# One-pass making of weight words, scores ahead of their bias, and plain copies that a planner may give to ScalarE or VectorE

## Chip, cores and metric

The kernel runs on one core of a Trainium2 chip. The metric is the device time of one execution in microseconds, 1084.62 us for the kernel before (median of three runs, 1083.74 to 1085.63).

## What is computed

The reference is a chain of an attention and two feed-forward layers:

```
scores = q @ k.T / sqrt(64) - slope[h] * dist, kept where the key is global or in the local window
x   = softmax(scores) @ v                    # 4 batches, 8 heads, 768 positions, head size 64
h   = x @ w_in
x   = (h * cos(h)) @ w_out                   # 3072 tokens, 512 -> 2048 -> 512
out = relu(x @ w2_in) ** 2 @ w2_out          # 3072 tokens, 512 -> 2048 -> 512
```

The four weight matrices arrive in double precision. The kernel makes a float32 word of each double from its two 32-bit halves, and splits the result into two fp16 parts, a high and a low one, so that TensorE multiplies in fp16 with three products for each block.

## The kernel before

The 3072 tokens are 24 tiles (T) of 128, four to each of six blocks (b). Layer 1 (m = 0) and layer 2 (m = 1) go block by block through a sequence of twelve stages, the first of which is layer 1 of block 0. That stage needs the attention of tiles 0 to 3 whole, and the weights of layer 1 pair by pair as it goes on.

`fast_path` does not issue instructions as it goes: each piece of work is an entry of a `Plan` with the engines that may do it, a cost, a due time and the buffers that it reads and writes. `Plan.run` then gives every engine its order, earliest due first, and a table `SHIFTS` moves the due times of attention tiles (A, P, X) and weights (W). An entry with one way has one engine; `split_lo` entries (the low fp16 part, a subtraction) may go to VectorE (DVE) or GpSimd (POOL). Each engine then works through its order strictly, so a late instruction holds up what stands behind it. Where the planner sees TensorE idle for over 0.9 us in the first 240 us, `idle_products` puts in products with a tile of zeros (`nought`).

What the change touches:

- `build_bias` (L494 to L519) makes a table of distances on DVE; `head_bias` (L523) makes from it the eight heads' biases on ScalarE (ACT).
- `group32` does the scores of four heads of tiles 0 to 3 in fp32: `add_bias` (L871) puts the bias into PSUM by a product with the identity, the score products (L788) add to it, `largest` takes the maximum (L878) and scales it (L882) on DVE, `expo_from` (L886) takes the exponentials on ACT, `diagonal` (L799 to L803) makes a diagonal of the reciprocal sums, products with it turn the tile (L816), ACT copies the turned tile out of PSUM (L821), products with v follow (L831), and ACT copies the result to SBUF (L840). There are eight such groups ahead of the first feed-forward product (L1125).
- `split_x`, `split_kq` and `weight` make a high part by an ACT copy to fp16 (L860, L696, L571; 1024 columns) and the low part by `split_lo` (L474).
- `decoded` loads 1 MB of doubles into one of two `raw` buffers (L558) and makes 1024 float32 words a partition from them: ACT's `magnitude` (L56), then three DVE passes, `join_steps`: a shift (L62), the low word's bits (L65), the sign (L68). The second and third read `raw`, so the buffer comes free after L68. 16 such units are made for layer 1 in the first 160 us and 16 for layer 2 later.

## Time and profile before

| | |
|---|---|
| median of the runs | 1084.62 us |
| the profiled execution | 1085.72 us, span 1084.0 us |
| TensorE (PE) busy | 1060.6 us, 98% of the span |
| DVE busy | 802.8 us, 74% |
| ACT busy | 752.9 us, 69% |
| POOL busy | 245.1 us, 23% |
| chain that ended last | PE 83%, DVE 11%, ACT 4% |

PE busy times are of pipelined matmuls with modelled ends, so a busy PE need not be doing useful products. In the rows further on, a stretch's PEclk is the clock that the throttle granted as a share of full speed, and in a timeline the bracket names the idle time before the instruction and what ended it.

### The profile page before, as it was taken

The numbers are of one execution on the slowest core, as the hardware profiler recorded it, in microseconds if no ns is written. First come the engines' busy times: TensorE is split into PE (matmuls) and PEld (weight loads), VectorE is DVE, ScalarE is ACT, GpSimd is POOL, SyncE is SP. The second block draws the span as 40 slices with busy tenths as digits, with TensorE's granted clock in tenths as the row PEclk, the third lists the DMA queues.
The fourth block names the chain that finished last, engine by engine and source line by source line (L and its number), as shares of the span: only waits on it lengthen the run. The fifth ranks groups of instructions, "written<-read, shape, count | busy, mean of one in ns | idle before, by whom it ended". The sixth has DMA issues, their size and how long they took to land.

```text
span 1084.0 us, 23236 instructions
## 1 busy us (share of the span) xinstructions
PE 1060.6 (98%) x9380; PEld 753.3 (69%) x9380; DVE 802.8 (74%) x1483; ACT 752.9 (69%) x1349; POOL 245.1 (23%) x192
## 2 busy tenths in 40 slices
...
GB/s 234 171 243 250 238 282 246 152 97 238 229 177 209 295 338 157 246 226 229 249 272 261 233 232 222 268 315 255 195 216 135 127 137 127 128 117 156 86 4 41
DMA packets 160687, 217.69 MB, mean 201 GB/s; under 512 B 110464, under 2 KB 110976, under 8 KB 159040
## 3 DMA queue, kind: packets, MB, share of 16 engines
...
## 4 chain that ended last, share of the span: by engine, by line
PE 83%; DVE 11%; ACT 4%; issue 1%; DMA 0%; DVEq 0%; SPq 0%; ACTq 0%
PE hps L1232 25%; PE ypps L1141 14%; PE hps L1125 13%; PE ypps L1368 11%; PE ypps L1438 7%; PE ypps L1183 7%; PE hps L922 2%; PE hps L983 2%; PE hps L1368 2%; DVE dec L65 1%; DVE nm L878 1%; DVE dec L68 1%; DVE dec L62 1%; DVE t L1426 1%; DVE xy L474 1%
## 5 line engine op out<-in xcount | busy, mean ns | idle before, releaser
L1232 PEld LDWEIGHTS <-ld 128*128 128x128 f16 x2400 | 234.0, 98 | 35.3 <-issue 2.6
L1232 PE MATMUL hps<-ys,ld 128*128 128x256 f16 x1680 | 195.1, 273 | 1.8 <-DVE t L1426 1.8
L1141 PE MATMUL ypps<-g,ld 128*128 128x512 f16 x768 | 177.8, 382 | 1.6 <-DVE g L474 1.6
L1125 PE MATMUL hps<-xy,w 128*128 128x512 f16 x768 | 174.5, 379 | 0.0
L1426 DVE TENSOR_TENSOR t<-hps,t 128x512 f32<-128x512 f32 x160 | 110.0, 688 | 66.4 <-PE hps L1232 64.3
L1141 PEld LDWEIGHTS <-ld 128*128 128x128 f16 x768 | 74.3, 98 | 90.2 <-issue 2.7
L1125 PEld LDWEIGHTS <-w 128*128 128x128 f16 x768 | 73.9, 98 | 86.2
L474 DVE TENSOR_TENSOR g<-t,g 128x512 f16<-128x512 f32 (+1 forms) x128 | 101.0, 793 | 26.0 <-ACT g L1209 25.2
L1209 ACT ACTIVATE g<-t 128x512 f16<-128x512 f32 x128 | 79.3, 622 | 23.5 <-DVE t L1165 21.8
L1183 PE MATMUL ypps<-g,ld 128*128 128x256 f16 x768 | 89.2, 273 | 0.5 <-DVE g L474 0.5
L1438 PE MATMUL ypps<-ld,g 128*128 128x512 f16 x384 | 89.5, 379 | 0.0
L1183 PEld LDWEIGHTS <-ld 128*128 128x128 f16 x768 | 75.0, 98 | 9.4 <-issue 0.6
L1423 ACT ACTIVATE t<-t 128x512 f32<-128x512 f32 x72 | 45.0, 624 | 48.9 <-DVE t L1426 48.6
L474 POOL TENSOR_TENSOR g<-t,g 128x512 f16<-128x512 f32 (+1 forms) x24 | 30.8, 1284 | 195.0 <-ACT g L1209 185.1
L1165 DVE SCALAR_TENSOR_TENSOR t<-t,hps 128x512 f32<-128x512 f32 x72 | 48.9, 682 | 31.9 <-ACT t L1163 31.9
L1161 ACT ACTIVATE t<-hps 128x512 f32<-128x512 f32 x72 | 42.7, 592 | 34.0 <-PE hps L1125 25.4
L1438 PEld LDWEIGHTS <-g 128*128 128x128 f16 x384 | 36.7, 98 | 37.1
L1163 ACT ACTIVATE t<-t 128x512 f32<-128x512 f32 x96 | 60.4, 629 | 2.6
L1258 ACT ACTIVATE t<-t 128x512 f32<-128x512 f32 x96 | 60.3, 628 | 2.5
L954 ACT ACTIVATE e<-e,nm 128x256 f32<-128x256 f32 (+1 forms) x128 | 52.7, 482 | 8.3 <-DVE nm L946 8.1
L946 DVE CUSTOM_DVE_ANT_0 e<-hps,bias 128x256 f32<-128x256 f32 (+2 forms) x128 | 43.2, 395 | 18.0 <-PE hps L922 17.9
L631 POOL TENSOR_TENSOR t<-t 128x256 f32<-128x256 f32 x18 | 16.4, 909 | 158.0 <-DVE x L631 157.9
...
## 6 DMA issues: line engine op xcount, KB each, us to landing
...
raw<-w SPq DMA_DIRECT2D x32, 1024.0 KB, 6.6
...
yd<-xy SPq DMA_DIRECT2D x6, 1024.0 KB, 5.8
xy<-yd SPq DMA_DIRECT2D x6, 1024.0 KB, 6.6
...
```

Source lines behind the costliest of these rows:

```text
L474: op.emit = lambda: eng[op.eng].tensor_tensor(out=out_f(), in0=src_f(), in1=hi_f(), op=ALU.subtract)
L954: nc.scalar.activation(out=at(e)[:, x, 0:W], in_=at(e)[:, x, 0:W], func=ACTF.Exp, bias=at(nm)[:, x:x + 1], scale=-1.0,)
L1125: nc.tensor.matmul(out=at(ps), lhsT=w_view(wt)[:, a, j % 2, k * 128:(k + 1) * 128], rhs=x_view(src)[:, c, k, :], start=(n == 0), stop=(n = ...
L1141: nc.tensor.matmul(out=at(y_ps[d]), lhsT=wv[:, a, d * 128:(d + 1) * 128], rhs=at(g)[:, c], start=(j == 0 and n == 0), stop=(j == NJ - 1 an ...
L1163: act(due + 1.2, 512, lambda: nc.scalar.activation(out=at(t), in_=at(t), func=ACTF.Square, scale=HALF_TURN), w=[t])
L1183: nc.tensor.matmul(out=at(y_ps[d])[:, 256 * n:256 * n + 256], lhsT=w_view(wt)[:, a, u, d * 128:(d + 1) * 128], rhs=at(g)[:, z, 256 * u:256 ...
L1209: act(due, 512, lambda: nc.scalar.activation(out=at(g)[:, 0], in_=at(t), func=ACTF.Copy), r=[t], new=[g])
L1232: nc.tensor.matmul(out=at(bank)[:, 256 * u:256 * u + 256], lhsT=wv(a, u, kk), rhs=sv(c, kk), start=(fresh and u == n == 0), stop=(last and ...
L1258: act(due, 512, lambda: nc.scalar.activation(out=at(t), in_=at(t), func=ACTF.Square), w=[t])
L1368: nc.tensor.matmul(out=at(bank)[:, 256 * half:256 * half + 256], lhsT=gv(home)[:, z, c0:c0 + 128], rhs=wv(a, u), start=(q == half == u == ...
L1426: dve(due, 0.7, lambda: nc.vector.tensor_tensor(out=at(t), in0=at(bank), in1=at(u), op=ALU.add), port=False, **k)
L1438: nc.tensor.matmul(out=at(y_ps[d]), lhsT=at(g)[:, z, 256 * u + d % 2 * 128:256 * u + d % 2 * 128 + 128], rhs=wv[:, a, u], start=(q == i == ...
```

## The change

- **Words.** The load lands one 16-bit word further into `raw`, so that the upper 16 bits of a double and the 32 bits below them each stand aligned. ACT's `top_half` (new L62) reads the upper 16 bits as bf16, scales, and writes an fp16 number into the upper half of a word of a new tile `top`, of which there is one; its lower halves are cleared once at the start. One DVE pass, `join` (new L69), ors in the middle bits. Shift and sign pass are gone. `raw` comes free after `join`.
- **Copies.** `cast` replaces the ACT copies named above (L571, L696, L821, L840, L860, the copies of attention probabilities and of g) by entries that the planner gives to ACT or to DVE (new L495 and L497). The scaling of the maximum is an entry of its own, `scaled`, for DVE, POOL or ACT (new L893, L891).
- **Beginning.** The scores are multiplied first and the bias added last, as two entries; heads 0, 1, 4 and 5 get their bias first; the cast of n_global and n_local comes two instructions later on DVE; the copies for the global keys wait for the last bias; the fp32 identity is gone.
- `SHIFTS` has other numbers. The counts of products, loads and stores are otherwise as they were.

```diff
@@ -49,29 +49,26 @@
 H_MOST = 3.0
-W_MAG = 2.0 ** -111
-def magnitude(nc, t, r):
-    nc.scalar.activation(out=t.bitcast(FP32), in_=r[:, :, 1].bitcast(FP32), func=ACTF.Abs, scale=W_MAG)
-def join_steps(nc, t, r):
-    return (
-        lambda: nc.vector.tensor_scalar(
-            out=t, in0=t, scalar1=3, scalar2=None, op0=ALU.logical_shift_left
-        ),
-        lambda: nc.vector.scalar_tensor_tensor(
-            out=t, in0=r[:, :, 0], scalar=29, in1=t, op0=ALU.logical_shift_right, op1=ALU.bitwise_or
-        ),
-        lambda: nc.vector.scalar_tensor_tensor(
-            out=t, in0=r[:, :, 1], scalar=-0x80000000, in1=t, op0=ALU.bitwise_and, op1=ALU.bitwise_or
-        ),
-    )
+INT16 = mybir.dt.int16
+UP = S_W ** 0.125
+def shifted(r, n):
+    return r.bitcast(INT16)[:, 1:4 * n + 1]
+def top_half(nc, t, r, n):
+    nc.scalar.activation(
+        out=t.bitcast(FP16).rearrange("p (c b) -> p c b", b=2)[:, :, 1],
+        in_=r.bitcast(BF16)[:, 4:4 * n + 4].rearrange("p (c b) -> p c b", b=4)[:, :, 0], func=ACTF.Copy, scale=UP)
+def join(nc, f, t, r, n):
+    nc.vector.scalar_tensor_tensor(
+        out=f, in0=r[:, 0:2 * n].rearrange("p (c b) -> p c b", b=2)[:, :, 1], scalar=13, in1=t,
+        op0=ALU.logical_shift_right, op1=ALU.bitwise_or)
 AHEAD = 2.0
@@ -82,51 +79,62 @@
...
-    ('A', 0, 0): 7.9,
+    ('A', 0, 0): -2.8,
...
-    ('W', 0, 0): -18.2,
+    ('W', 0, 0): -6.6,
...
+EITHER = 10.0
+BEGIN = 1.3
+RATE = 320.0
@@ -337,7 +346,7 @@
                                 held.append(item)
                                 break
                         elif ok and e == "DVE":
-                            k = o.due + (SHARED if len(o.ways) > 1 else 0.0) + (BESIDE if port and beside else 0.0)
+                            k = o.due + (0.0 if len(o.ways) == 1 else EITHER if o.ways[0][0] == "ACT" else SHARED) + (BESIDE if port and beside else 0.0)
                             if pick is None or k < key:
                                 pick, key = (o, way), k
                             if key <= o.due:
@@ -427,7 +436,7 @@
     kinds = dict(
-        raw=(2, [128, 1024, 2], INT32), ld=(9, [128, 1024], FP32), ys=(4, [128, 2048], FP16), kq=(3, [128, 2, 2, HR, 128], FP16), 
...
@@ -477,6 +485,20 @@
     def act(due, n, fn, **k):
         return plan.add((("ACT", (n + 230) / 1200, False),), due, fn, **k)
+    def cast(due, n, out, src, psum=False, **k):
+
+        us = (n + 150) / 960 if psum else (n / 2 + 150) / 960
+        o = plan.add((("ACT", (n + 230) / 1200, False), ("DVE", us, not psum)), due, None, **k)
+
+        def fn():
+            if o.eng == "ACT":
+                nc.scalar.activation(out=out(), in_=src(), func=ACTF.Copy)
+            else:
+                nc.vector.tensor_copy(out=out(), in_=src())
+
+        o.emit = fn
+        return o
+
     def own(b, first):
@@ -513,10 +533,13 @@
         nc.vector.tensor_scalar(out=t, in0=rel, scalar1=0.0, scalar2=BIG, op0=ALU.is_lt, op1=ALU.mult)
         nc.vector.tensor_tensor(out=t, in0=t, in1=rel, op=ALU.add)
+        nc.vector.tensor_copy(out=nf, in_=n_raw[:, :, 0])
...
         nc.vector.scalar_tensor_tensor(out=t, in0=col, scalar=nf[:, 1:2], in1=t, op0=ALU.max, op1=ALU.min)
+
+        nc.gpsimd.memset(slots["top"][0], 0)
...
@@ -553,22 +576,20 @@
     def decoded(m, e, jj, due):
-        t, raw = new("dec"), new("raw")
-        r = lambda: at(raw)
+        f, t, raw = new("dec"), new("top"), new("raw")
         dma(due - 12, 1024, lambda: nc.sync.dma_start(
-            out=r().rearrange("p (u a) b -> p u (a b)", u=2),
-            in_=w[m, e, 2 * jj:2 * jj + 2].bitcast(INT32).rearrange("u p c -> p u c")), new=[raw])
-        act(due - 7, 1140, lambda: magnitude(nc, at(t), r()), r=[raw], new=[t])
-        for n, us in enumerate((0.69, 1.22, 1.22)):
-            dve(due - 5.6 + 1.3 * n, us, lambda n=n: join_steps(nc, at(t), r())[n](), r=[raw] if n else [], w=[t])
-        return t
+            out=shifted(at(raw), 1024).rearrange("p (u c) -> p u c", u=2),
+            in_=w[m, e, 2 * jj:2 * jj + 2].bitcast(INT16).rearrange("u p c -> p u c")), new=[raw])
+        act(due - 7, 1024, lambda: top_half(nc, at(t), at(raw), 1024), r=[raw], new=[t])
+        dve(due - 5.6, 1.22, lambda: join(nc, at(f), at(t), at(raw), 1024), r=[t, raw], new=[f])
+        return f
     def weight(m, e, jj, due):
         t = decoded(m, e, jj, due)
         o = new("w1" if m == e == 0 else "ld")
         f = lambda: at(t).bitcast(FP32).rearrange("p (u c) -> p u c", u=2)
         ov = lambda: w_view(o)
-        act(due - 2.2, 1024, lambda: nc.scalar.activation(out=ov()[:, 0], in_=f(), func=ACTF.Copy), r=[t], new=[o])
+        cast(due - 2.2, 1024, lambda: ov()[:, 0], f, r=[t], new=[o])
         split_lo(o, due - 1.2, lambda: ov()[:, 1], f, lambda: ov()[:, 0], 1024, [t], [o])
         if m == 0:
...
@@ -780,18 +800,21 @@
         rows = (slice(0, D), slice(D, 128))
         def scores():
-            add_bias(ps, g, adds)
             for i in range(2):
                 c = 2 * g + i
-                for o, kk, c0, n in keys:
+                for n0, (o, kk, c0, n) in enumerate(keys):
                     for r in range(2):
                         nc.tensor.matmul(
                             out=at(ps[r])[:, 256 * i + o:256 * i + o + n], lhsT=f4(f)[rows[r], 1, c, :],
-                            rhs=f4(kk)[rows[r], 0, c, c0:c0 + n], start=False, stop=True, skip_group_check=True,
+                            rhs=f4(kk)[rows[r], 0, c, c0:c0 + n], start=(i == n0 == 0), stop=False, skip_group_check=True,
                         )
-        plan.add((("PE", 2.0, False),), s, scores, r=reads, new=ps, lag=0.3, after=[biased[h] for h in heads])
+        k = dict(part=reads) if T == g == 0 else dict(r=reads)
+        plan.add((("PE", 1.3 if t else 0.65, False),), s, scores, new=ps, lag=0.3, **k)
+        plan.add((("PE", 0.65, False),), s + 0.5, lambda: add_bias(ps, g, adds, last=True), w=ps, lag=0.3,
+                 after=[biased[h] for h in heads])
         dve(s + 1, 1.4 * W / 256, lambda: largest(ps, nm, W), port=False, r=ps, new=[nm])
+        scaled(nm, s + 2.5)
         act(s + 3, 1980 if t else 1460, lambda: expo_from(ps, e, nm, W, sums), r=ps, w=[nm], new=[e, sums], tab="exp")
         op = dve(s + 5, 1.1, None, r=[sums], new=[diag])
@@ -818,8 +841,7 @@
                     )
             plan.add((("PE", 1.2, False),), s + 7 + k, turned, r=[e, diag], new=[tp], lag=0.3)
-            act(s + 8 + k, 512, lambda tp=tp, pt=pt: nc.scalar.activation(
-                out=at(pt), in_=at(tp), func=ACTF.Copy), r=[tp], new=[pt])
+            cast(s + 8 + k, 512, lambda pt=pt: at(pt), lambda tp=tp: at(tp), psum=True, r=[tp], new=[pt])
             pts.append(pt)
         blocks = [v32[T - 1], v32[T]] if t else [v32[T]]
...
-    def add_bias(ps, g, adds):
+    def scaled(nm, due):
+
+        o = plan.add((("DVE", 0.17, True), ("POOL", 0.2, True), ("ACT", 0.21, False)), due, None, w=[nm])
+
+        def fn():
+            if o.eng == "ACT":
+                nc.scalar.activation(out=at(nm), in_=at(nm), func=ACTF.Copy, scale=-SCALE)
+            else:
+                eng[o.eng].tensor_scalar(out=at(nm), in0=at(nm), scalar1=-SCALE, scalar2=None, op0=ALU.mult)
+
+        o.emit = fn
+
+    def add_bias(ps, g, adds, last=False):
         for r in range(2):
@@ -870,7 +902,7 @@
             for n, (c0, c1, b0) in enumerate(adds):
                 nc.tensor.matmul(
                     out=p[:, :, c0:c1], lhsT=ident, rhs=bias[:, h0:h0 + 2, b0:b0 + c1 - c0],
-                    start=(n == 0), stop=False, skip_group_check=True,
+                    start=(n == 0 and not last), stop=last, skip_group_check=True,
                 )
...
-        nc.vector.tensor_scalar(out=at(nm), in0=at(nm), scalar1=-SCALE, scalar2=None, op0=ALU.mult)
...
@@ -1532,9 +1563,10 @@
         fill(3, at_(13))
-    dist_of = dve(0.0, 4.0, build_bias, r=[], after=())
-    for h in range(H):
-        biased.append(act(4.0 + PAIR * (h // 2), 320, lambda h=h: head_bias(h), after=[dist_of]))
+    dist_of = dve(0.0, 5.4, build_bias, r=[], after=())
+    biased = {}
+    for n, h in enumerate((0, 1, 4, 5, 2, 3, 6, 7)):
+        biased[h] = act(4.0 + PAIR * (n // 2), 215, lambda h=h: head_bias(h), after=[dist_of])
     for T in range(BT):
         attend32(T)
```


Three places show what it does to the orders. The first is TensorE's very first instructions; `hps` are PSUM banks, `ld` loaded tiles, `ident` the identity. Before:

```order
L871 LDWEIGHTS ident
L871 MATMUL hps_138<-bias,ident 128x2x224
L871 LDWEIGHTS ident
L871 MATMUL hps_138<-bias,ident 128x2x32
L871 LDWEIGHTS ident
L871 MATMUL hps_139<-bias,ident 128x2x224
L871 LDWEIGHTS ident
L871 MATMUL hps_139<-bias,ident 128x2x32
L788 MATMUL hps_138<-ld_72 128x128
L788 MATMUL hps_139<-ld_72 128x128
L788 MATMUL hps_138<-ld_70,ld_72 128x128
L788 MATMUL hps_139<-ld_70,ld_72 128x128
```

and now:

```order
L807 MATMUL hps_139<-ld_71 128x128
L807 MATMUL hps_140<-ld_71 128x128
L807 MATMUL hps_139<-ld_71 128x128
L807 MATMUL hps_140<-ld_71 128x128
L903 LDWEIGHTS ident
L903 MATMUL hps_139<-bias,ident 128x2x96
L903 LDWEIGHTS ident
L903 MATMUL hps_139<-bias,ident 128x2x32
L903 LDWEIGHTS ident
L903 MATMUL hps_140<-bias,ident 128x2x96
L903 LDWEIGHTS ident
L903 MATMUL hps_140<-bias,ident 128x2x32
```

The bias products of the first group stood ahead of its scores and now stand behind them, and the first group is that of tile 0 (keys of its own tile alone) where it was tile 1's.

The second is DVE around the first units of weights, some 30 instructions in; `w_0` is the high and low part of the first weights, `sm` sums, `xy` the attention's result, `t` a turned tile. Before:

```order
L62 TENSOR_SCALAR dec_109<-dec_109 128x1024
L65 SCALAR_TENSOR_TENSOR dec_109<-raw_68,dec_109 128x1024
L878 TENSOR_REDUCE nm_94<-hps_140 128x2
L878 TENSOR_REDUCE nm_94<-hps_141 128x2
L882 TENSOR_SCALAR nm_94<-nm_94 128x4
L68 SCALAR_TENSOR_TENSOR dec_109<-raw_68,dec_109 128x1024
L799 TENSOR_SCALAR sm_97<-sm_97 128x4
L802 RECIPROCAL sm_97<-sm_97 128x4
L803 TENSOR_TENSOR t_123<-ident_197,sm_97 128x512
L703 SCALAR_TENSOR_TENSOR v_87<-ld_73,v_87 128x8x64
L1547 COPY v_87<-vg_90 32x16x64
```

and now:

```order
L69 SCALAR_TENSOR_TENSOR dec_110<-raw_69,top_68 128x1024
L497 CAST w_0_112<-dec_110 128x1024
L822 TENSOR_SCALAR sm_96<-sm_96 128x4
L825 RECIPROCAL sm_96<-sm_96 128x4
L826 TENSOR_TENSOR t_120<-ident,sm_96 128x512
L482 TENSOR_TENSOR w_0_112<-dec_110,w_0_112 128x1024
L69 SCALAR_TENSOR_TENSOR dec_111<-raw_70,top_68 128x1024
L910 TENSOR_REDUCE nm_93<-hps_141 128x2
L910 TENSOR_REDUCE nm_93<-hps_142 128x2
L497 COPY xy_107<-ypps_145 128x2x128
L482 TENSOR_TENSOR w_1_113<-dec_111,w_1_113 128x1024
L497 COPY t_124<-ypps_146 128x512
```

One `join` stands for the three passes of a unit, and between the groups' instructions there are now copies to fp16 (`w_0`) and out of PSUM (`xy`, `t`) that ACT did. No scaling of `nm` stands there.

The third is ACT's first work; `vg` and `kg` are the global values and keys, `bias` the biases of the eight heads. Before:

```order
L753 ACTIVATE vg_90<-ld_71 32x8x64
L523 ACTIVATE bias<-dist 128x320 x8
L696 ACTIVATE kq_83<-ld_73 128x1024
L748 ACTIVATE kg_89<-ld_70 128x128
L701 ACTIVATE v_86<-ld_75 128x8x64
L886 ACTIVATE e_99,sm_95<-hps_138,nm_91 128x256 x2
L886 ACTIVATE e_99,sm_95<-hps_139,nm_91 128x256 x2
L886 ACTIVATE e_100,sm_96<-hps_140,nm_92 128x128 x2
```

and now:

```order
L546 ACTIVATE bias<-ys_80 128x320 x8
L773 ACTIVATE vg_91<-ld_73 32x8x64
L917 ACTIVATE e_100,sm_96<-hps_139,nm_92 128x128 x2
L917 ACTIVATE e_100,sm_96<-hps_140,nm_92 128x128 x2
L720 ACTIVATE v_87<-ld_75 128x8x64
L768 ACTIVATE kg_90<-ld_71 128x128
L891 ACTIVATE nm_93<-nm_93 128x4
L917 ACTIVATE e_101,sm_97<-hps_141,nm_93 128x128 x2
```

The exponentials of the first group now follow two instructions after the biases; a copy of `kq` went to DVE, the copies of `v` and `kg` stand behind the first group, and a scaling of `nm` is ACT's.

## Rows read from the trace of the kernel before

**Rows 1.** The page, part 1: busy time, share of the span and instructions.

```profile
PE 1060.6 (98%) x9380; PEld 753.3 (69%) x9380; DVE 802.8 (74%) x1483; ACT 752.9 (69%) x1349; POOL 245.1 (23%) x192
```

**Rows 2.** Stretches: length; busy PE, PEld, DVE, ACT, POOL; PEclk; DMA share; GB/s.

```profile
10.00:61.00 51.00, 48.20 (x523) 36.80 (x522) 48.88 (x83) 44.69 (x115) 7.23 (x3) 1.00 0.62 205
61.00:136.00 75.00, 74.53 (x580) 37.81 (x579) 70.18 (x90) 67.92 (x107) 23.78 (x14) 1.00 0.88 245
136.00:140.00 4.00, 1.81 (x30) 1.04 (x28) 4.00 (x5) 2.71 (x6) 1.35 (x1) 1.00 0.80 279
140.00:143.60 3.60, 3.60 (x10) 1.25 (x10) 3.41 (x7) 3.56 (x7) 3.54 (x2) 0.53 0.70 282
...
513.00:517.00 4.00, 2.39 (x24) 1.38 (x22) 4.00 (x22) 2.86 (x8) 0.00 (x0) 1.00 0.86 330
```

**Rows 3.** Timeline of the first 14 us: start, duration, engine, line, operation [idle before].

```profile
3.51 0.17 DVE L504 CAST nf<-n_raw 128x2 f32<-128x2 int32 x1 [1.65 <-DMA n_raw<-n]
...
4.47 0.39 DVE L516 TENSOR_SCALAR x<-x,nf 128x320 f32<-128x320 f32 x1
...
5.71 0.55 DVE L519 SCALAR_TENSOR_TENSOR dist<-x,nf,dist 128x320 f32<-128x320 f32 x1
...
6.30 2.98 ACT L523 ACTIVATE bias<-dist 128x320 bf16<-128x320 f32 x8 [0.44 <-DVE dist L519]
...
8.62 0.59 PE L871 MATMUL hps<-bias,ident 128*128 128x448 bf16 x2 [0.85 <-ACT bias L523]
...
11.15 0.61 PE L871 MATMUL hps<-bias,ident 128*128 128x192 bf16 x4
...
11.52 1.28 DVE L878 TENSOR_REDUCE nm<-hps 128x2 f32<-128x512 f32 x2
...
13.10 0.47 ACT L886 ACTIVATE e<-hps,nm 128x256 f32<-128x256 f32 x1 [1.12 <-DVE nm L882]
```

**Rows 4.** Groups by line, DVE, 10 to 61 us: busy, mean ns.

```profile
L65 DVE SCALAR_TENSOR_TENSOR dec<-raw,dec 128x1024 int32<-128x1024 int32 x5 | 7.9, 1583 | 0.1
L68 DVE SCALAR_TENSOR_TENSOR dec<-raw,dec 128x1024 int32<-128x1024 int32 x5 | 6.1, 1219 | 0.0
...
L62 DVE TENSOR_SCALAR dec<-dec 128x1024 int32<-128x1024 int32 x5 | 3.4, 686 | 0.0
...
L882 DVE TENSOR_SCALAR nm<-nm 128x4 f32<-128x4 f32 x10 | 2.3, 232 | 0.3
```

**Rows 5.** Groups by line, ACT, 10 to 61 us.

```profile
L821 ACT ACTIVATE t<-ypps 128x512 f32<-128x512 f32 x14 | 8.5, 622 | 2.8 <-PE ypps L816 2.7
...
L571 ACT ACTIVATE w<-dec 128x1024 f16<-128x1024 f32 x3 | 3.1, 1072 | 0.0
L840 ACT ACTIVATE xy<-ypps 128x256 f32<-128x256 f32 x8 | 3.0, 405 | 0.3 <-PE ypps L831 0.3
```

**Rows 6.** Timeline, 57 to 66 us, DVE and PE around the first product.

```profile
58.84 1.22 DVE L474 TENSOR_TENSOR xy<-xy,xy 128x1024 f16<-128x1024 f32 x1
...
61.05 2.75 PE L1125 MATMUL hps<-xy,w 128*128 128x512 f16 x12
```

**Rows 7.** Timeline, 18 to 22 us, POOL beside DVE.

```profile
18.47 2.54 POOL L474 TENSOR_TENSOR kq<-ld,kq 128x1024 f16<-128x1024 f32 x1 [15.51 <-ACT kq L696]
...
19.06 3.03 DVE L65 SCALAR_TENSOR_TENSOR dec<-raw,dec 128x1024 int32<-128x1024 int32 x1
```

**Rows 8.** Groups by line, DVE, 61 to 140 us.

```profile
L1165 DVE SCALAR_TENSOR_TENSOR t<-t,hps 128x512 f32<-128x512 f32 x13 | 8.8, 681 | 3.1 <-ACT t L1163 3.1
...
L1000 DVE TENSOR_TENSOR x<-hps,sm 128x256 f32<-128x256 f32 x6 | 2.5, 425 | 0.6
```

**Rows 9.** Groups by line, ACT, 61 to 140 us.

```profile
L993 ACT ACTIVATE sm<-hps 128x4 f32<-128x4 f32 x8 | 1.3, 159 | 1.3 <-PE hps L983 1.3
```

**Rows 10.** DMA issues to 165 us: count, KB each, median us to landing.

```profile
raw<-w SPq DMA_DIRECT2D x18, 1024.0 KB, 5.9
...
pt<-p SPq DMA_TRANSPOSE x8, 5.5
```

148 lines of the change are left out of this document (77 added, 71 removed).

## Prediction

> **What bounds the kernel now.** I read the page first: TensorE is busy 98% of the span [rows 1]. A kernel in that state can only get faster where TensorE is not doing useful products, so the next view was busy time by stretch, and within the stretches the timeline and the groups by line.
>
> The first feed-forward product starts at 61.05 us [rows 6]. Ahead of it TensorE counts as busy for 48.20 of the 51 us after 10 us [rows 2], but with small attention products and products of zeros; the same products could be done far sooner if their inputs were there. In that stretch DVE is busy 48.88 of 51 us and ACT 44.69 [rows 2]: DVE sets the pace, ACT is close behind. The last DVE work before the first product is the low part of x, from 58.84 to 60.06 us [rows 6], in a queue with no holes.
>
> From 61 to 136 us TensorE has 74.53 of 75 us and DVE still 70.18 [rows 2]. Then DVE is late once: from 136 to 140 us TensorE is busy 1.81 of 4 us, and right after that its granted clock is 0.53 for 3.6 us, so nearly all of that stretch at 1.2 GHz in place of 2.4 [rows 2]. That costs 2.2 us of idle time and 3.6 x 0.47 = 1.7 us of slow clock, 3.9 us. Later there is one more visible hole, 513 to 517 us, 1.6 us [rows 2]. So the prize is the beginning, a matter of 61 us, and some 5 us of holes behind it; what a faster DVE or ACT wins elsewhere is worth nothing under a busy TensorE.
>
> **The beginning of the beginning.** The cast of n_global and n_local waits for its DMA until 3.51 us and ends at 3.68; two DVE passes that do not need it ran after it, since the first that needs it starts at 4.47 [rows 3]. They now stand ahead of the cast, so the table of distances ends about 0.8 us sooner, at 5.5 in place of 6.26. The eight biases take 2.98 us, 0.37 each [rows 3]. The first group needed heads 0, 1, 4 and 5, the sixth bias in the old order: its second pair of bias products starts at 8.62 [rows 3], and the score products follow. Now four biases are enough (5.5 + 1.5 = 7.0), the scores are already in PSUM, and only four short bias products remain, 0.61 us by the same four of tile 0 [rows 3]. The first maximum can start near 7.8 instead of 11.52 [rows 3]: 3.7 us sooner. On ACT the first exponential came at 13.10 behind a copy of kq and of v; now it follows the last bias (8.5) and the copy of vg, near 9.2, 3.9 us sooner. I take 3.7 us.
>
> **DVE ahead of the first product.** I counted both orders up to the low part of x. Gone: five shifts (3.4 us) and five sign passes (6.1 us) [rows 4]; nine of ten scalings of the maximum, 9 x 0.232 = 2.1 us [rows 4]; one of seven low parts, 1.2 us [rows 6], which POOL takes. The pass that stays, `join`, has the shape and operands of L65, whose undisturbed length I take as that of L68, 1.22 us [rows 4]. Together 12.8 us less. New: four copies to fp16 of 1024 columns; no row shows one, and the nearest are the one-input pass L62, 0.69 us, and the two-input pass L68, 1.22 us [rows 4]. I take 0.69, because a copy has one input: 2.8 us (4.9 at the other end; at 0 it cannot be, since it has to pass 1024 columns). Four PSUM copies of 512 columns at 0.68 and five of 256 at 0.425 by the nearest PSUM readers [rows 8]: 2.7 + 2.1 us. Together 7.6 us more. Net 5.2 us less (3.1 at the dear end).
>
> **ACT ahead of the first product.** Copies of 1024 columns fall from ten to seven (3 x 1.07), of 512 from fourteen to ten (4 x 0.62), of 256 from eight to three (5 x 0.405) [rows 5]: 7.7 us less. Eight scalings of four numbers come in at 0.16 each by a four-number ACT row [rows 9]: 1.3 us. `top_half` has the width of the pass it replaces; I cost the exchange at nothing. ACT falls by 6.4 us, so it does not become the bound, and DVE's 5.2 counts.
>
> **Moved DMAs.** On SP a 512 KB kq load now goes out second, three places earlier, and the first 1 MB of weights some three issues later, 1.5 us; its first reader on ACT stands behind two groups of exponentials in either order, so I cost it at nothing.
>
> **The sum.** 3.7 + 5.2 = 8.9 us if DVE stays as dense as now. It will not quite: POOL takes two more low parts ahead of the first product, and POOL work beside DVE costs it (a POOL pass of 2.54 us made a DVE pass last 3.03 in place of 1.22 [rows 7], 1.8 us; the next passes pay less, so 2 us for the two), and with less work a queue in strict order waits more often for its inputs, 1 us. I take 6 us: the first product at 55. Behind it, DVE loses shift and sign pass of the eleven units that are left, 11 x (0.69 + 1.22) = 21 us, and gets back eight copies of 1024 columns and seven of 512 at 0.69 and 0.42, 8.4 us, and some 4 us of low parts and maxima in the order up to the end of that stage, of about 80 us. That covers most of the hole at 136 us; I take 2.5 of the 3.9 us, and nothing at 513 us. 8.5 us off 1085.72 of the profiled execution is 1077.2; that execution is 1.1 us above the median of the runs, so the forecast for a median is **1076 us**.
>
> **A rule that speaks against the change.** The trace shows DVE and POOL in each other's way [rows 7]. The Trainium skill, page "SBUF — State Buffer", section "Who interferes with whom", says that copies and casts within SBUF can run in a mode that takes both ports, and that DVE then excludes GpSimd for the whole instruction, or waits for it. By that rule each cast that meets a POOL pass waits it out, and the moved copies, harmless on ACT, are dear on DVE; the second rival is what that would give.
>
> **Rivals.**
>
> 1. *Everything arrives.* DVE stays dense, the holes go: 8.9 + 3.9 + 1.6 = 14.4 us, a median of 1070. For it: DVE has 9 us less in the 80 us behind the first product. Against it: a strict queue has so far not been hole-free, and POOL has more to do. Chance 0.15.
> 2. *Casts and POOL collide.* Each of the four casts ahead of the first product loses the 1.8 us of rows 7, 7.2 of the 8.9 us, and the hole at 136 us stays, as 15 casts more lie ahead of it: 1.7 us gained, 1083. It decides from about one collision per cast on. Against it: five L65 lost 1.8 us in total (mean 1583 ns, 1219 undisturbed [rows 4]), so one in five was hit. Chance 0.10.
> 3. *One `top`.* With a single tile ACT's `top_half` must wait until DVE has joined the unit before, and behind it in ACT's queue stand exponentials that the groups wait for. Between two joins DVE's order has a diagonal, a low part and a cast, about 3 us; two such waits are 6 us of the 8.9: 1081.7. Chance 0.09.
> 4. *The shifted load is slower* (the other side). The destination now starts two bytes off a word. The trace shows no such load; 1 MB as before lands in 5.9 us, and transposes move their 0.5 MB in 5.5 us [rows 10], the dear end, about 11 us. From 61 to 136 us the DMA engines are 0.88 busy at 245 GB/s, 18 MB, of which some 8 MB are these loads [rows 2, 10], so they hold about 0.4 of the time. The queue becomes the bound once they cost some 30% more; at twice the cost the stretch needs 0.88 + 0.4 = 1.28 of its 75 us, 21 us more, less the 6 us of the beginning: 1099. Against it: the rows stay 4 KB long. The Trainium skill, page "DMA: Bandwidth & Descriptors", section "How a descriptor splits into AXI transactions", counts one transaction more for a run that starts off its grid, as an estimate 17 for 16, 6%, which would stay hidden; no run here shows it. Chance 0.06.
>
> **How the numbers follow.** My forecast has 0.60, with a range of its own of 1072 to 1080 (first product between 52 and 58 us, the hole filled or not). The range for 8 in 10 takes in rival 1 below and rivals 2 and 3 in part above: 1068 to 1083; rival 4 lies outside. A measurement tells this kernel from no change at about 0.2%, 2.2 us. Faster by more: the forecast, rival 1, most of rival 3 and a little of rival 2, 0.60 + 0.15 + 0.07 + 0.02 = 0.84. Within: the rest of 2 and 3, less 0.01, 0.09. Slower: rival 4 and that 0.01, 0.07.
>
> **What would show it.** Right: the first maximum near 8 us, the first feed-forward product near 55, the DVE copies of 1024 columns near 0.7 us, no stretch at half clock near 130 us, and TensorE's time from the first product on otherwise as before. Wrong: a first product at 59 or later with casts well over 1 us (rival 2) or with ACT idle in front of `top_half` (rival 3); weight loads landing in 10 us and SP or TensorE waiting for them (rival 4); a new hole behind 60 us that takes back what the beginning gave.

## The result and the profile after

The changed kernel takes **1068.12 us** (median of four runs, 1067.98 to 1068.15), the kernel before, in the same session, 1084.18 us. The ratio is 0.985, with a 95% interval of 0.9833 to 0.9867: 16 us faster. The forecast was 1076.0, 8.6 us below the runs shown; the time lies at the lower end of the range. The sign was right, the size was half of what came.

The page, part 1, of the changed kernel, against [rows 1]:

```profile
PE 1052.6 (99%) x9371; PEld 750.3 (70%) x9371; DVE 791.2 (74%) x1502; ACT 708.3 (66%) x1273; POOL 256.9 (24%) x194
```

PE's idle time is down, ACT is busy 45 us less, DVE only 12: its passes went, and ACT's copies came.

The changed kernel's profiled execution is 17.6 us shorter than that of the kernel before, and two times divide this. The first feed-forward product starts at 52.28 us (new L1156) where it started at 61.05 [rows 6], 8.8 us sooner. From there to the end of the last product it takes 1008.65 us in place of 1017.34, another 8.7. I call the stretch up to the first product **ahead** and the one after it **behind**.

Ahead, the timeline (start, duration) answers to [rows 3] and [rows 6]:

```profile
5.11 0.55 DVE L540 SCALAR_TENSOR_TENSOR ys<-x,nf,ys 128x320 f32<-128x320 f32 x1
...
8.05 0.74 DVE L910 TENSOR_REDUCE nm<-hps 128x2 f32<-128x256 f32 x2
...
9.11 0.36 ACT L917 ACTIVATE e<-hps,nm 128x128 f32<-128x128 f32 x1
```

```profile
52.28 2.75 PE L1156 MATMUL hps<-xy,w 128*128 128x512 f16 x12
...
59.80 2.75 PE L1156 MATMUL hps<-xy,w 128*128 128x512 f16 x12 [0.56 <-DVE norms L1603]
```

The distances end at 5.66 us, the first maximum starts at 8.05 in place of 11.52, the first exponential at 9.11 in place of 13.10. Behind the first product, PE now stands still once near it, 0.56 us at 59.2.

From the first maximum to the first product, in the columns of [rows 2], first the kernel before and then the changed one:

```profile
11.52:61.05 49.53, 46.73 (x511) 35.54 (x509) 47.78 (x83) 43.97 (x113) 7.28 (x3) 1.00 0.60 198
```

```profile
8.05:52.28 44.23, 44.23 (x517) 34.70 (x515) 40.83 (x73) 40.81 (x114) 10.97 (x5) 1.00 0.75 264
```

The stretch is 5.3 us shorter. DVE works 7.0 us less in it and idles 3.40 us where it idled 1.75; ACT works 3.2 us less. Both are now equally full.

Behind, the stretches of the changed kernel answer to [rows 2]; the last row of the fence is one of 500 us, and under it stands the same stretch of the kernel before:

```profile
8.00:52.30 44.30, 44.30 (x518) 34.75 (x517) 40.90 (x73) 40.88 (x114) 10.97 (x5) 1.00 0.75 264
52.30:136.00 83.70, 83.14 (x622) 41.89 (x621) 73.03 (x98) 72.80 (x116) 29.73 (x15) 1.00 0.95 277
136.00:140.00 4.00, 4.00 (x73) 2.57 (x72) 3.30 (x13) 2.40 (x5) 0.42 (x1) 1.00 1.00 388
140.00:143.60 3.60, 3.60 (x24) 1.83 (x23) 1.98 (x4) 3.57 (x6) 1.01 (x2) 1.00 0.85 197
500.00:1000.00 500.00, 497.94 (x4762) 421.33 (x4761) 369.63 (x703) 303.14 (x557) 126.92 (x98) 1.00 0.63 196
```

```profile
500.00:1000.00 500.00, 495.74 (x4718) 415.55 (x4716) 362.86 (x691) 322.99 (x591) 136.08 (x109) 1.00 0.65 204
```

The hole at 136 us and the half clock after it are gone (4.00 of 4.00 us busy, clock 1.00). From 500 to 1000 us PE is idle 2.1 us where it was 4.3. One more thing was in the trace before, which busy time hides; this is the view of one line, the products of zeros behind the first feed-forward product:

```profile
L1755 PE MATMUL ypps<-bias,nought x7: 379/379/390, 118.4 to 130.4; 128*128 128x512 bf16 x7
```

There were seven, and there are none now; at 0.23 us each (13 of them take 2.98 us in the changed kernel's timeline at 47 us) they are 1.6 us. So the 8.7 us are: idle time of PE 4.3 (0.47, 2.19 and 4.26 before, 0.56 and 2.06 now), half clock 1.7 as the prediction had it, zeros 1.6, and 1.1 that I did not locate.

The DVE groups of the changed kernel from 8 to 52 us (busy, mean ns), against [rows 4] and [rows 8], and ACT's new first pass:

```profile
L69 DVE SCALAR_TENSOR_TENSOR dec<-raw,top 128x1024 int32<-128x1024 int32 x5 | 6.1, 1218 | 0.2 <-ACT nm L891 0.2
...
L482 DVE TENSOR_TENSOR xy<-xy,xy 128x1024 f16<-128x1024 f32 x2 | 4.0, 2020 | 0.2 <-ACT xy L495 0.2
L497 DVE COPY t<-ypps 128x512 f32<-128x512 f32 x4 | 2.6, 680 | 0.0
L497 DVE COPY xy<-ypps 128x256 f32<-128x256 f32 x5 | 2.1, 417 | 0.0
...
L497 DVE CAST w<-dec 128x1024 f16<-128x1024 f32 x1 | 0.7, 694 | 0.0
L497 DVE CAST kq<-ld 128x1024 f16<-128x1024 f32 x1 | 0.7, 685 | 0.0
...
L497 DVE CAST p<-e 128x1024 f16<-128x1024 f32 x1 | 0.7, 683 | 0.0
```

```profile
L62 ACT ACTIVATE top<-raw 128x1024 f16<-128x1024 bf16 x5 | 6.9, 1372 | 0.0
```

### The profile page after: what moved, and what is told of

The parts are those of the page before. It is cut to its first block, busy times and chain, and to the rows that moved or that the text cites. A ratio compares the mean times of both kernels' runs of the same rounds, so it can differ in the third digit from the quotient of the medians.

```text
span 1066.4 us, 23185 instructions
## 1 busy us (share of the span) xinstructions
PE 1052.6 (99%) x9371; PEld 750.3 (70%) x9371; DVE 791.2 (74%) x1502; ACT 708.3 (66%) x1273; POOL 256.9 (24%) x194
## 3 DMA queue, kind: packets, MB, share of 16 engines
q8 instruction: 74, 1.21, 0.5%
## 4 chain that ended last, share of the span: by engine, by line
PE 90%; DVE 3%; issue 1%; ACT 1%; DMA 0%; DVEq 0%; ACTq 0%
PE hps L1263 26%; PE ypps L1172 16%; PE hps L1156 15%; PE ypps L1399 12%; PE ypps L1214 8%; PE ypps L1469 6%; PE hps L1015 2%; PE hps L953 2%; PE hps L1399 2%; DVE ld L482 1%; DMA ld<-w 0%; PE hps L1599 0%; DVE g L482 0%; PE hps L968 0%; DVE t L1457 0%
## 5 line engine op out<-in xcount | busy, mean ns | idle before, releaser
L1156 PE MATMUL hps<-xy,w 128*128 128x512 f16 x768 | 173.8, 379 | 0.6 <-DVE norms L1603 0.6
L1156 PEld LDWEIGHTS <-w 128*128 128x128 f16 x768 | 73.9, 98 | 87.2 <-issue 0.7
L482 DVE TENSOR_TENSOR g<-t,g 128x512 f16<-128x512 f32 (+1 forms) x122 | 98.6, 812 | 15.6 <-ACT g L495 14.3
L482 POOL TENSOR_TENSOR g<-t,g 128x512 f16<-128x512 f32 (+1 forms) x30 | 43.1, 1438 | 164.4 <-DVE g L497 87.0
L495 ACT ACTIVATE g<-t 128x512 f16<-128x512 f32 x81 | 50.4, 624 | 24.8 <-DVE t L1196 23.7
L482 POOL TENSOR_TENSOR p<-e,p 128x1024 f16<-128x1024 f32 x15 | 35.2, 2348 | 86.9 <-DVE p L497 30.2
```

Source lines behind the costliest of these rows:

```text
L482: op.emit = lambda: eng[op.eng].tensor_tensor(out=out_f(), in0=src_f(), in1=hi_f(), op=ALU.subtract)
L495: nc.scalar.activation(out=out(), in_=src(), func=ACTF.Copy)
L1156: nc.tensor.matmul(out=at(ps), lhsT=w_view(wt)[:, a, j % 2, k * 128:(k + 1) * 128], rhs=x_view(src)[:, c, k, :], start=(n == 0), stop=(n = ...
```

## The experiments

Each kernel was timed against the kernel before on the same chip, at other times than the first two rows of this table, where before's median lay between 1083.9 and 1085.0; "first" is the start of the first feed-forward product, "behind" the time from there to the end of the last product, both from the profiled execution, which can lie some us off the median where runs scatter (e1, e5, e16, e17).

| kernel | median us | ratio to before, 95% | first | behind |
|---|---|---|---|---|
| before | 1084.18 | 1 | 61.05 | 1017.3 |
| changed | 1068.12 | 0.985 (0.9833 to 0.9867) | 52.28 | 1008.7 |
| e1 three passes, all units | 1112.05 | 1.0252 (1.0235 to 1.0269) | 64.29 | 1038.8 |
| e5 three passes, first five units | 1087.12 | 1.002 (1.0009 to 1.0031) | 64.22 | 1013.5 |
| e6 three passes, other 27 units | 1094.53 | 1.0089 (1.0069 to 1.0109) | 52.16 | 1035.1 |
| e2 copies on ACT | 1080.69 | 0.9964 (0.995 to 0.9978) | 56.88 | 1017.3 |
| e3 old beginning | 1071.21 | 0.9875 (0.9858 to 0.9891) | 55.23 | 1008.7 |
| e4 old table | 1078.09 | 0.9938 (0.9921 to 0.9954) | 61.84 | 1008.7 |
| e7 before, new table | 1100.30 | 1.0139 (1.0122 to 1.0156) | 64.72 | 1028.3 |
| e8 changed, no table | 1074.08 | 0.9898 (0.9882 to 0.9915) | 56.31 | 1010.5 |
| e9 before, no table | 1092.12 | 1.007 (1.0054 to 1.0087) | 60.23 | 1024.7 |
| e10 as e8, three passes | 1095.17 | 1.0096 (1.0079 to 1.0113) | 58.80 | 1029.7 |
| e11 as e8, copies on ACT | 1074.76 | 0.9908 (0.9891 to 0.9924) | 56.95 | 1011.4 |
| e14 before, join put in | 1085.62 | 1.001 (1.0001 to 1.002) | 61.71 | 1016.8 |
| e16 before with join, planned | 1084.06 | 0.9992 (0.9981 to 1.0002) | 56.20 | 1018.1 |
| e17 as e16, no table | 1087.52 | 1.0028 (1.0016 to 1.0039) | 63.56 | 1018.3 |
| e18 as e17, new constants | 1079.82 | 0.9957 (0.9943 to 0.997) | 62.02 | 1010.6 |
| e12 changed, rows moved just ahead of the product | 1071.76 | 0.9884 (0.9868 to 0.9901) | 50.61 | 1013.8 |
| e13 as e12, weight's low part on DVE | 1072.90 | 0.9898 (0.9882 to 0.9915) | 50.77 | 1014.4 |
| e15 as e13, maximum behind its products | 1067.98 | 0.9849 (0.9836 to 0.9863) | 50.62 | 1010.1 |

### Parts taken out of the changed kernel, its order kept

**Passes.** In e1 each `join` is three DVE passes again; e5 does it at the first five units alone, e6 at the other 27.

```diff
+    low = r[:, 0:2 * n].rearrange("p (c b) -> p c b", b=2)[:, :, 1]
+    nc.vector.tensor_scalar(out=f, in0=low, scalar1=13, scalar2=None, op0=ALU.logical_shift_right)
+    for i in range(2):
-    nc.vector.scalar_tensor_tensor(out=f, in0=low, scalar=13, in1=t, ...)
+        nc.vector.scalar_tensor_tensor(out=f, in0=low, scalar=13, in1=t, ...)
```

> The changed kernel with its order kept as it is, but each join made in three DVE passes again (a shift of 0.69 us and twice the two-input pass of 1.22 us): 1.9 us more of DVE at each of the 32 weight units, the words come out the same. Theory A (DVE's passes set the first product and the holes behind it): five units stand ahead of the first product, so it comes 5 x 1.9 = 9.6 us later, near 62; behind it eleven more units put 21 us on DVE up to 144 us, where DVE has about 14 us left, so holes come back near 130 to 140 us, another 5 us with a stretch at half clock: 1068 + 9.6 + 5 = 1083 or more. Theory B (the new order table, or the copies that moved, gave most of it): the passes find room, the first product comes at most 4 us later and the time is under 1075.

> As the run with three DVE passes at all 32 units, but only at the five units whose joins stand ahead of the first feed-forward product; the other 27 keep the one pass. There the first product came 12.0 us later (64.3 in place of 52.3) and the time was 44 us longer. Theory A (the five passes ahead set the first product, and what follows has room): the first product again near 64, and the rest as in the changed kernel, 1068 + 12 = 1080. Theory B (a late beginning also throws the order behind it out of step): the first product near 64, and over 1085 with holes at 60 to 150 us. Theory C (the five are absorbed): under 1074.

> The complement: one pass at the first five units, three passes at the other 27. Theory A (DVE behind the first product has no more room than about 14 us up to 144 us, against eleven units x 1.9 = 21 us): the first product at 52 to 54, holes of 6 us or more at 80 to 160 us, the sixteen later units spread over 550 us and mostly hidden; 1068 + 10 to 32 = 1078 to 1100, together with the first five the 44 us. Theory B (the old passes behind the first product were hidden, and the 8.7 us that the changed kernel won there come from its order): under 1072.

e1 took 1112, 44 us more than the changed kernel and 28 more than the kernel before. e5 took 19 us more, e6 26; together 45, so the two halves add up. Theory A held in kind and was far too small in e1, where I had given DVE some room that it did not have; e6 is inside its range. e5 is above Theory A's 1080 and has the signs of Theory B: over 1085, and a hole behind 60 us. In e5's profiled execution, which is 17 us longer than that of the changed kernel (its runs scatter from 1084.4 to 1089.0), the first product came 12 us later, as expected, and the other 5 us (behind) are a hole and what followed it. These are the two stretches of e5, the columns those of [rows 2]:

```profile
64.60:67.74 3.14, 0.01 (x2) 0.00 (x1) 3.14 (x3) 2.30 (x2) 3.14 (x2) 0.91 0.65 185
67.74:71.00 3.26, 2.92 (x7) 0.95 (x7) 3.26 (x2) 0.00 (x0) 1.92 (x1) 0.57 1.13 317
```

After one product of the first block PE stood still from 64.60 to 67.74, until DVE had made the low part of x, and over the next 3.3 us its granted clock was 0.57. In e6, DVE is full from 61 to 136 us, and PE has lost 8 of 75 us:

```profile
61.00:136.00 75.00, 66.65 (x473) 32.34 (x473) 72.95 (x96) 51.09 (x79) 19.22 (x11) 0.95 0.79 232
```

**Copies.** In e2 every `cast` is emitted on ACT at its place in the order.

```diff
         def fn():
-            if o.eng == "ACT":
-                nc.scalar.activation(out=out(), in_=src(), func=ACTF.Copy)
-            else:
-                nc.vector.tensor_copy(out=out(), in_=src())
+            nc.scalar.activation(out=out(), in_=src(), func=ACTF.Copy)
```

> The changed kernel with its order kept, but all plain copies emitted on ACT, those too that were given to DVE. Ahead of the first product ACT gets four copies of 1024 columns, four PSUM copies of 512 and five of 256, 4 x 1.07 + 4 x 0.60 + 5 x 0.39 = 8.6 us more, in a stretch where it is busy 44 of 48 us; DVE loses 7.4 us there. Theory A (the passes did it, but only because the copies balance the two engines): ACT becomes the bound and the first product comes 4 to 9 us later, 56 to 61; the time is 1073 to 1080. Theory B (DVE alone is the bound, the copies are a burden to it): the first product comes sooner or at the same time, and the time is 1068 or less.

1080.7, 12.6 us more and just over Theory A's range: 4.6 ahead, as Theory A had it, and 8.6 behind. From 8 to 52 us ACT is busy 41.4 of 44 us and DVE 33.5, where in the changed kernel each is busy 40.6:

```profile
8.00:52.00 44.00, 42.33 (x466) 33.54 (x466) 33.53 (x58) 41.44 (x118) 6.60 (x4) 1.00 0.67 252
```

**Beginning and table.** e3 emits the bias products ahead of the scores, the cast of n first and the heads in their old order; e4 plans the changed kernel with the old `SHIFTS`, and e7 the kernel before with the new one.

```diff
-        plan.add((("PE", 1.3 if t else 0.65, False),), s, scores, new=ps, lag=0.3, **k)
-        plan.add((("PE", 0.65, False),), s + 0.5, lambda: add_bias(ps, g, adds, last=True), w=ps, lag=0.3,
+        def both():
+            add_bias(ps, g, adds)
+            scores()
...
+        plan.add((("PE", 1.3 if t else 0.65, False),), s, lambda: None, new=ps, lag=0.3, **k)
+        plan.add((("PE", 0.65, False),), s + 0.5, both, w=ps, lag=0.3,
```

> The changed kernel with its order kept, but with the old beginning: the cast of n ahead of the two passes that do not need it, the biases in the order of the heads, and in each group of the float32 attention the bias products ahead of the score products, together where the bias products now stand. Theory A (the beginning gives what was counted, 3.7 us, and DVE's queue hands it on whole): the first maximum near 11.5 us in place of some 8, the first feed-forward product near 56, the time 1068 + 3.7 = 1072. Theory B (DVE's work decides, and a late beginning is caught up in the queue): under 1 us.

> The changed kernel planned with the old table of shifts of due times; everything else of the change stays. Theory A (less work on DVE gives the time, the table only smooths): 1068 to 1074. Theory B (the table gives what my sum could not explain, some 8 us): 1075 or more, with the holes behind 60 us back.

> The kernel before, planned with the new table of shifts and nothing else of the change. Theory A (a table fits the kernel it was made for, as the changed kernel lost 10 us under the old one): slower than 1084, by 5 to 15 us. Theory B (the new table is the better one for both): 1076 to 1082.

e3 lost 3.1 us, all of it ahead (first 55.23, behind 1008.7 as in the changed kernel). That is Theory A's time, but not its path: the first maximum starts at 9.51 us, 1.5 us later than in the changed kernel, not near 11.5, and the other 1.5 us are lost at later groups. e4 lost 10 us, and again all of it ahead. Neither theory had that: the holes behind did not come back (Theory B's sign), yet the time was over Theory A's 1074. With the other kernel's table the kernel before loses 15 us against the 1085.0 that it took beside it (e7). So e4 and e7 say only that a table fits the order it was made for.

### The parts without a table

To keep the table out of it, I planned with `SHIFTS = {}`: e8 the changed kernel, e9 the kernel before; e10 is e8 with three passes at every join and a cost of 3.13 us for them in the planner, e11 is e8 with `cast` given one way, ACT.

```diff
-        dve(due - 5.6, 1.22, lambda: join(nc, at(f), at(t), at(raw), 1024), r=[t, raw], new=[f])
+        dve(due - 5.6, 3.13, lambda: join(nc, at(f), at(t), at(raw), 1024), r=[t, raw], new=[f])
...
-        o = plan.add((("ACT", (n + 230) / 1200, False), ("DVE", us, not psum)), due, None, **k)
+        o = plan.add((("ACT", (n + 230) / 1200, False),), due, None, **k)
```

> The changed kernel with an empty table, every due time as the formulas give it. Theory A (less DVE work keeps the queues loose, so that order matters little): 1078 to 1085, no worse by much than with the table of the other kernel (1078). Theory B (the order is worth more than the passes): over 1090, with a first product past 65 us.

> The kernel before, planned with an empty table; its counterpart, the changed kernel with an empty table, took 1074.1. Theory A (the change is worth what it does to the engines, and each table then gave its own kernel some us): 1090, the same 16 us above its counterpart, give or take 6. Theory B (half of the 16 us came out of the tables): within 8 us of 1074, so at most 1082.

> The changed kernel with an empty table, three DVE passes at each of the 32 joins, and the planner told so (3.13 us in place of 1.22), so that it orders the rest around them. With the order kept as it was, the passes cost 44 us. Theory A (DVE is short of time up to about 150 us, whatever the order): 10 to 25 us above 1074, 1084 to 1099. Theory B (the 44 us came from an order that was planned for shorter joins): under 6 us, at most 1080.

> The changed kernel with an empty table, with all plain copies planned on ACT alone. With the order kept, that cost 12.6 us. Theory A (ACT and DVE are both nearly full ahead of the first product, so the copies must be shared whatever the order): 5 to 13 us above 1074, 1079 to 1087. Theory B (a planner that knows of it finds room): under 3 us.

e8, at 1074.1, was better than either theory: the table gives the changed kernel 6 us, 4 of them ahead, and the kernel before 8. Without tables the change is worth 18.0 us (1092.1 to 1074.1), with each kernel's own table 16.1: Theory A of e9. The three passes cost 21 us even where the planner knows of them (Theory A of e10), 19 of them behind. So everything but the one-pass join, put together, gains nothing: e10, which has it all, is 3 us slower than e9, which has none of it. The shared copies are here worth nothing that these runs can tell: 0.7 us, the runs 1074.2 to 1075.5 against 1074.0 to 1074.5 (Theory B of e11). The 12.6 us of e2 would then be the price of an order that counted on DVE for them; no run plans the copies on ACT alone with the table.

### The join alone in the old kernel

e16 and e17 plan the kernel before anew with the join, with the old table and with none (the first hunk below); in e14 the four entries of the plan stay, the first two DVE ones issue nothing and the third issues `join`, so that DVE's order is the old one; a first pass on ACT that would come ahead of the join of the unit before now stands right behind it. The fp32 identity and the tile of distances make room for `top`, as in the change. e18 adds to e17 the planner's new constants (the second hunk).

```diff
-        act(due - 7, 1140, lambda: magnitude(nc, at(t), r()), r=[raw], new=[t])
-        for n, us in enumerate((0.69, 1.22, 1.22)):
-            dve(due - 5.6 + 1.3 * n, us, lambda n=n: join_steps(nc, at(t), r())[n](), ...)
+        act(due - 7, 1024, lambda: top_half(nc, at(t), at(raw), 1024), r=[raw], new=[t])
+        dve(due - 5.6, 1.22, lambda: join(nc, at(f), at(t), at(raw), 1024), r=[t, raw], new=[f])
...
+BEGIN = 1.3
+RATE = 320.0
-        return (("DVE", (n + 151) / 960, True), ("POOL", (n * 2.6 + 100) / 1200, True))
+        return (("DVE", (n + 151) / 960, True), ("POOL", (n * 2.3 + 200) / 1200, True))
```

> The kernel before in its own order and with its own table, the one-pass join alone put in: the raw load two bytes off, the new first pass on ACT, the join in the place of the third DVE pass, and the first two passes left out; copies, scalings and beginning as before. There is one tile top, so that a first pass on ACT that stood ahead of the join of the unit before now comes right behind it. Theory A (the passes are the gain, in any order): the first product 6 to 9.6 us sooner than 61.0, the hole and the half clock at 136 to 143 us gone, 1069 to 1076. Theory B (the lighter DVE is worth something only with the copies moved to it and a new order): 1078 to 1084.

> The kernel before with the join alone, as in e14, but planned anew: one DVE pass of 1.22 us in the planner, top as a tile of its pool, the old table of shifts, all copies on ACT, scalings on DVE, the old beginning. Theory A (the fixed order gave the time back): the first product 5 us or more sooner than 61.0, 1069 to 1078. Theory B (ACT sets the pace once DVE is light, the join needs the copies shared): DVE idle for 10 us or more ahead of the first product, 1080 to 1086.

> The same with an empty table; without the join that was 1092.1, and the changed kernel with an empty table 1074.1, or 1074.8 with all copies on ACT. Theory A (the join is nearly all of the gain where the order is planned for it): 1075 to 1080, what is left to 1074 being the beginning (3.1 us in e3). Theory B (the copies and scalings carry as much): 1083 to 1092.

> As e17 (the kernel before with the join alone, planned anew with an empty table, 1087.5), with the planner's new constants: loads begin at 1.3 us, 320 KB per us in place of 300, and a low part on POOL priced at 2.13 us in place of 2.3 (1024 columns). Theory A (a plan that knows the loads better carries much of the 12.7 us): 1075 to 1081, and the first product near 57. Theory B (the constants only shuffle the order, the beginning and the scalings carry it): 1084 to 1090.

e14 gave nothing: 1085.6, above both theories. DVE had lost its passes and simply waited. This is its row from 10 to 61 us, and the first lines of what its queue waited for in that stretch (us in total, times, longest):

```profile
10.00:61.00 51.00, 47.45 (x520) 36.66 (x519) 39.23 (x73) 44.54 (x115) 5.47 (x3) 1.00 0.60 210
```

```profile
DVE nm L885 <- PE hps L795: 3.5, 3, 2.0
DVE kq L470 <- ACT kq L703: 3.4, 1, 3.4
DVE sm L806 <- ACT e L893: 3.2, 5, 1.0
DVE dec L69 <- ACT top L62: 1.4, 1, 1.4
DVE ld L470 <- ACT ld L580: 1.3, 1, 1.3
```

DVE is busy 39.2 of 51 us where [rows 2] had 48.9, PE no more than there, ACT 44.5 as there. The wait for kq began before 10 us and stands in the kernel before as well; of the others PE ended some 3.7 us and ACT 6.8.

Planned anew with the old table (e16), the first product comes at 56.20 us, 4.9 us sooner, with every copy still on ACT. This is e16 from its first maximum to its first product:

```profile
11.46:56.20 44.74, 42.44 (x501) 33.76 (x502) 37.08 (x72) 41.88 (x111) 6.53 (x3) 0.96 0.70 231
```

The 44.7 us are nearly the 44.2 of the changed kernel. But this profiled execution, 1081.56 us, is one of the three fastest of ten, which scatter from 1081.5 to 1085.4. Their median is that of the kernel before, inside Theory B's range, and what takes the gain back in the slower ones no trace here shows. Without a table (e17) the join took 4.6 us off e9 (Theory B). In the profiled executions its first product came 3.3 us later, and the gain is behind, 6.4 us.

What e17 lacks against the changed kernel shows in the rows of e17, e18 and e11, the stretches 10 to 61 and 500 to 1000 us of each, in this order:

```profile
10.00:61.00 51.00, 46.58 (x477) 36.53 (x477) 38.57 (x71) 44.29 (x114) 4.42 (x2) 0.97 0.66 225
500.00:1000.00 500.00, 492.97 (x4680) 412.90 (x4679) 367.51 (x693) 319.24 (x584) 128.61 (x102) 1.00 0.64 202
```

```profile
10.00:61.00 51.00, 46.18 (x504) 35.84 (x505) 41.28 (x73) 45.88 (x115) 6.59 (x3) 1.00 0.70 230
500.00:1000.00 500.00, 498.47 (x4758) 419.30 (x4757) 368.41 (x711) 322.74 (x591) 127.47 (x98) 1.00 0.65 203
```

```profile
10.00:61.00 51.00, 49.85 (x537) 37.69 (x536) 41.68 (x67) 47.01 (x119) 6.38 (x4) 1.00 0.69 236
500.00:1000.00 500.00, 498.47 (x4765) 420.03 (x4764) 365.20 (x708) 319.60 (x587) 123.50 (x96) 1.00 0.64 202
```

From e17 to e18 only constants of the planner changed, and PE's idle time from 500 to 1000 us falls from 7.0 to 1.5 us. Behind, e18 is 7.7 us shorter, and 7.7 us lie between the medians (Theory A, though the first product stayed at 62.0 and did not come near 57; ahead there are another 1.5 in the profiled executions, but that of e17 was 1.5 us above its median). This idle time follows the constants in every kernel here: 4.3 to 7.0 us in the six with the old ones (before, e7, e9, e14, e16, e17), 1.3 to 2.1 us in the fourteen with the new ones, 2.1 even with three passes (e1). From e18 to e11 the beginning and the scalings came in: behind 1010.6 and 1011.4, nearly the same; the first product 5.1 us sooner, with the first maximum 4.2 us sooner (11.14 to 6.98 us).

So, without tables, this is the order in which I added the parts, each step a run: join −4.6, constants −7.7, beginning and scalings −5.1, copies −0.7, together −18.0 before rounding. It is one order among several: taken out last, the join is worth 21 (e10), put in first, 4.6. No run changes the constants alone in the kernel before or in the changed one.

### The last microseconds ahead of the first product

In the changed kernel a POOL pass stands beside the low parts of x. These are two rows of DVE's timeline (the second holds both low parts) and one of POOL's:

```profile
47.57 1.22 DVE L69 SCALAR_TENSOR_TENSOR dec<-raw,top 128x1024 int32<-128x1024 int32 x1
49.04 3.96 DVE L482 TENSOR_TENSOR xy<-xy,xy 128x1024 f16<-128x1024 f32 x2 [0.25 <-ACT xy L495]
```

```profile
47.59 3.19 POOL L482 TENSOR_TENSOR ld<-dec,ld 128x1024 f16<-128x1024 f32 x1
```

POOL's pass ran to 50.78, and the first low part of x, which could start at 49.04, ended 1.1 us after that, 2.83 us long in place of 1.21. e12 moved the pass away, brought the second copy of x forward on ACT and took out nine products of zeros. `put` moves an entry of the finished order behind another; names stand here in place of the entries' numbers, and the lines are shortened.

```diff
     idle = idle_products(order)
+    idle[of_the_last_scores], idle[of_the_first_product] = 9, 0   # products of zeros, were 13 and 5
+    put(second_copy_of_x, behind=first_copy_of_x)            # ACT
+    put(low_part_of_weight, behind=next_low_part_of_p)       # POOL; in e13 and e15 to DVE, behind the low parts of x
+    put(store_of_weight, behind=low_part_of_weight)          # SP
+    put(maximum_of_lengths, behind=join_after_x)             # DVE, e13; in e15 behind its products
```

> The changed kernel with a few rows moved just ahead of the first feed-forward product: on ACT the second copy of x stands behind the first one, ahead of the four exponentials; on POOL the low part of a second-layer weight stands behind the next low part of p, so that no POOL pass runs beside the low parts of x; its store goes one place later on SP; nine products of zeros in place of thirteen, and none in place of five, ahead of the first product. Theory A (POOL beside DVE stretched the first low part of x from 1.21 to 2.83 us on the path): that low part takes 1.2 us, the first product comes at 50 to 51 in place of 52.3, the time is 1066 to 1067.5. Theory B (what waits behind, the exponentials and the second-layer weight, takes it back): first product earlier, the time 1068 to 1070.

> As the run before with rows moved just ahead of the first feed-forward product, but the low part of the second-layer weight goes to DVE, right behind the low parts of x, in place of later on POOL (there DVE's next join waited 4.2 us for it), and the maximum over the lengths of x stands one place earlier on DVE, ahead of the next low part of a weight. Theory A (the POOL pass beside the low part of x held the first product back, and nothing else stands behind it): the first product near 50.6, the join behind it without a wait, no hole at 59 us, 1068.1 less 1.7 less up to 0.6: 1065.8 to 1067. Theory B (what follows is paced by something else, so that an earlier first product only makes the next hole longer): 1067.5 to 1069.

> As e13, but the maximum over the lengths of x stands right behind the products that it reads; in e13 it stood ahead of them, and TensorE waited 5 us for it. Theory A (the POOL pass beside the low part of x is on the path): the first product near 50.8, no hole of more than 1 us up to 64 us, 1066 to 1067. Theory B (the time goes into the next wait): 1067.5 or more.

All three had the first product at 50.6 to 50.8, and none was faster; e12 and e13 were slower than either theory had them. In e12 the low parts of x ran in 2.36 us, but the next join had to wait until the moved POOL pass had read the buffer that it writes:

```profile
48.92 2.36 DVE L482 TENSOR_TENSOR xy<-xy,xy 128x1024 f16<-128x1024 f32 x2 [0.24 <-ACT xy L495]
...
56.70 3.14 DVE L69 SCALAR_TENSOR_TENSOR dec<-raw,top 128x1024 int32<-128x1024 int32 x1 [4.23 <-POOL ld L482]
```

In e13 I had put a maximum ahead of the products that it reads (it reads other data there), and TensorE waited 5 us for it. e15 has neither fault, and is the changed kernel's equal (1067.98 against 1068.12). PE's timeline there:

```profile
50.62 2.75 PE L1156 MATMUL hps<-xy,w 128*128 128x512 f16 x12 [0.33 <-ACT e L917]
...
55.61 2.75 PE L1156 MATMUL hps<-xy,w 128*128 128x512 f16 x12 [1.34 <-ACT e L917]
```

The product came 1.7 us sooner, and the next one of its line waits 1.34 us until ACT's exponentials are done. Theory B of e15: the collision was on the path, and right behind it stood a wait of nearly the same size. The 1.7 us are those of three moves made at once; the low parts of x took 1.6 us less (3.96 to 2.36). No version here beats the changed kernel.

## Why the prediction was right, and where it was wrong

**The beginning, 3.7 us: right in size, half of it by another way.** The first maximum came 3.5 us sooner. e3, which takes the order of biases and scores back, loses 3.1 us, but only 1.5 of them at the first maximum. The rest comes at later groups, whose scores wait for their biases again: a maximum at 17.32 us in the changed kernel is 2.25 us late in e3, one at 34.46 us 2.7 us. The 2 us of the first maximum that e3 leaves in place go with what it does not undo, such as tile 0's group ahead of tile 1's and the cast of kq on DVE; no run parts these.

**DVE ahead of the first product, 5.2 us: the prices right, the match with 5.3 luck.** The copies cost 0.683 to 0.694, 0.680 and 0.417 us where I took 0.69, 0.68 and 0.425. The stretch from the first maximum to the first product became 5.3 us shorter, but as 7.0 us less of work and 1.7 us more of waiting. Of the four copies of 1024 columns that I had charged to it one stands at 6.18 us, ahead of the first maximum; the rest of the surplus I did not locate.

**The step "I take 6 us" of 8.9: wrong, by 2.8.** The 2 us that I took off for POOL beside DVE were in the trace before already: five L65 stretched by 1.8 us together [rows 4]. Now they are 1.6 (the two low parts of x, 2 x (2.02 − 1.21)) and 0.4 elsewhere. So the exchange cost 0.2, and I had charged it again. DVE's waits rose by 1.7, where I had 1. Its work, without the stretched passes, fell by some 7.1, where I had 5.2. These three together, 1.8 − 0.7 + 1.9, with 0.2 less at the beginning, are the 2.8.

**The step "2.5 of the 3.9 us, and nothing at 513 us": wrong, by 6.** Behind the first product 8.7 us were won. All of the 3.9 went, and with it 1.6 us of products of zeros, which I had counted as a busy TensorE, and 2.2 us of idle time between 500 and 1000 us. For the 3.9 the lighter DVE is shown to be needed: e6 puts the passes back, and PE idles 8 of 75 us there. My figure for DVE (21 us off, 12 back) no run tests by itself. What I had no term for are the planner's constants, two of which (`BEGIN`, `RATE`) stood in the diff. The 2.2 us go with them, as that idle time is low in every kernel with the new ones and high in every kernel with the old. e17 to e18 gives them 7.7 us, but there they also give back 2.8 us of the same idle time that the join had added (4.3 in e9, 7.0 in e17). How much of the 8.7 is theirs in the two kernels compared stays open.

**"DVE sets the pace, ACT is close behind": right of the work, incomplete without the order.** By that sentence the join alone should have won at least its 5 us ahead in the old kernel. In the old order it won nothing (e14): ACT, 44.5 us busy as before, and PE ended DVE's idle time. Planned anew it won 4.9 us ahead in the execution profiled (e16), with all copies on ACT. So a new order is what the sum took for granted. A freed ACT, which the prediction secured by "it does not become the bound", is not shown to be needed: without a table, all copies on ACT cost 0.7 us (e11).

**The exchange on ACT "at nothing", and "ACT falls by 6.4 us": too small and too large.** `top_half` takes 1.37 us; L56, which it replaces, took 1.16 as the mean of its fourteen from 10 to 140 us. That is 0.2 us a unit, 1 us in the five ahead. From the first maximum to the first product ACT's busy time fell by 3.2 us, half of what I had counted. It did no visible harm: ACT is as full as DVE there, 40.81 and 40.83 of 44.23 us.

**The rivals.** The first, everything arrives, is what came, and more: 14.4 us there, 16.1 measured, though DVE did not stay dense (3.4 us idle) and two holes are left between 500 and 1000 us, 0.66 us at 521.62 and 1.05 at 618.92. The second did not happen ahead of the first product: none of the four casts there met a POOL pass. Two lost 0.9 us or more later, of 88 in all. One began at 107.58 us:

```profile
106.52 2.13 POOL L482 TENSOR_TENSOR w<-dec,w 128x1024 f16<-128x1024 f32 x1 [0.36 <-ACT sm L1025]
...
107.58 1.35 DVE L497 CAST g<-t 128x512 f16<-128x512 f32 x1
```

It took 1.35 us in place of 0.42 and ended 0.28 us after POOL. That agrees with the rule in the Trainium skill, page "SBUF — State Buffer", section "Who interferes with whom", by which the one that comes second waits for the whole of the other. This meeting cost 0.9 us, the other (at 293.42 us, 1.91 us long) 1.5, and there were too few to decide. The third: ACT was idle for 0.0 us in front of `top_half` in the group shown above. The fourth: the shifted load lands in 6.4 us by the page's list of DMA issues (6.6 for the 32 loads before; up to 165 us 6.2 against the 5.9 of [rows 10]), so the dear end of [rows 10] falls. The estimate of 17 transactions for 16, by the Trainium skill, page "DMA: Bandwidth & Descriptors", section "How a descriptor splits into AXI transactions", can be neither seen nor excluded in these times.
